# First stage of a spectral filter and mixer kernel: whole folds by class, 32-column rests, and four filters' scans moved into the filter stage

## The chip, the cores and the metric

The kernel runs on one core of a Trainium2 chip. The metric is the device time of one execution in microseconds (us). The kernel before took 1020.65 us, the median of three runs.

## The reference

The input x has S = 2048 tokens (rows) and D = 640 channels (columns). Two kinds of layer alternate, each used twice with the same weights:

```python
def _A_ref(x, w_r, w_i):                 # x: (2048, 640)
    X = rfft2(x)                          # (2048, 321), complex
    X = X * (w_r + 1j * w_i)              # the filter
    return irfft2(X, s=(S, D))
def _B_ref(x, w1, b1, w2, b2):
    h = _layernorm(x)
    u = gelu(einsum("bsd,sf->bdf", h, w1) + b1)     # F = 1728
    return (einsum("bdf,fs->bds", u, w2) + b2).transpose(0, 2, 1)
x = x + _A_ref(_layernorm(x), A_w_r, A_w_i)
x = x + _B_ref(_layernorm(x), ...)
x = x + _A_ref(_layernorm(x), A_w_r, A_w_i)
x = x + _B_ref(_layernorm(x), ...)
```

## The kernel before, in words

The two-dimensional transform is split: along the tokens into 16 × 128 and along the channels into sums and differences of the two halves of a row (a fold), so that cosine and sine tables are multiplied with half as many columns. Values that have to be exact to float32 are held as two float16 numbers, a high and a low part (names that end in h and l), and multiplied in three products (`mm3`).

The stages are written one after the other: `a0_first`, the first stage; `a1`, the filter stage; `a2` and `b1st`, the way back and the first mixer product; then the same for the second layer.

**First stage, `a0_first`.** Sixteen tiles of 128 tokens by 640 channels. For a tile: the statistics of the normalization (`stats`, VectorE: bn_stats twice, then bn_aggr, which writes mv); the centering (`center`, ScalarE, writes one half of zz); a first fold across the row on GpSimd (`diff` and `total`, two instructions of 320 columns on zz); a second fold on VectorE, `adds` and `subs`, which take zz and write F. After it GpSimd copies the end columns that have no partner (`ends`). F is multiplied with the table tm on TensorE in float32 (`product`); tm is the table scaled on ScalarE by the tile's 1/sigma (`scaled`). The result is in PSUM (ps) and split into s1h on ScalarE and s1l on VectorE. A product waits for the copy of the ends, for tm and for s1l of the tile four before it, which frees PSUM. The first four tiles are folded one by one, the other twelve in pairs (m = i // 2). In `product` fill products on a tile of ones (`self.warm`) stand ahead of each pair. An F row is laid out as four blocks of 128 columns and then one block of 128 with four rests of 32: `adds` writes blocks 0 and 3 in one instruction and their rests in a second (helper `each`), `subs` blocks 1 and 2 and their rests. So there are five products of 128 columns a tile, the fifth over all rests.

The filters w (16 groups of 128 x 642 numbers) are loaded in this stage a first time, and ScalarE squares each and sums it (`scan`, tiles jw and xq); the sums give the scale sx.

**Filter stage, `a1`.** Sixteen groups g: the forward product D(g) on TensorE (24 products), its split ph (ScalarE) and pl (VectorE), the row products R and S for two groups at a time, the multiplication with the filter ta and tb (VectorE; they read w and sx), the sums c0 and c1 (GpSimd), xh and xl, the backward products J and I, and the write into Y. From g = 4 on (G0) D needs a stacked operand stk, which is built by transfers through DRAM: s1h and s1l are stored to rest[0] and rest[1] (`store`, line 684), and then read back in another layout (`stack`, lines 690 and 692). The filters are loaded again (`wfetch`, line 698), at most four ahead. `scale_x` makes sx in four steps, on TensorE, VectorE, TensorE and VectorE: the first product (eye, xq) is called X0 here, the second X2.

**What sets the order.** The class `Plan` takes steps with an engine, an assumed duration, the steps that come before, a rank and an earliest time (at), works out an order and issues the instructions in it; VectorE, ScalarE, GpSimd and TensorE keep it. `SEQ1` is the order of TensorE's steps in the filter stage in both layers, written by hand; `SHIFT` moves the rank of single steps. Transfers stand on SyncE's queue in the order that the tile scheduler gives them, behind the semaphores that they need.

Line 56 (58 in the changed kernel) is the wrapper through which all pinned instructions are issued, so nearly all rows of the compute engines bear that line; they are told apart by the tiles.

Of the kernel before, what the change touches and what calls it, by code (L numbers as in the profile page):

```python
# [11 lines left out]
BF16 = mybir.dt.bfloat16  # L12
AF = mybir.ActivationFunctionType
ALU = mybir.AluOpType
# [19 lines left out]
YS = 2.0 ** -14  # L34
PG = 0, 14
WARM = 12, 6
SHIFT = {('y', 1): 2.6, ('xh2', 0): 2.3, ('c0', 1): -1.5, ('w', 1): 2.9, ('xl2', 1): -2.4, ('store', 0): -4.6, ('yh', 0): -2.5, ('yl', 0): 0.4, ('ta', 0): -5.1}
SEQ1 = (
    "D0 D1 S0 D2 D3 D4 S2 I0 D5 I1 S4 D7 I2 D6 I3 S6 D10 I4 D9 D8 I5 "
    "S8 I6 D11 I7 S10 D12 I8 D13 D14 S12 I10 I9 S14 D15 I11 I12 S15 I13 W14 I14 W15 I15"  # L40
)
I32 = mybir.dt.int32
# [97 lines left out]
class Layers:  # L140
# [298 lines left out]
    def a0_first(self, pw):  # L439
# [41 lines left out]
            (eng or G).tensor_tensor(two(e, 1, 161), two(e, 1, 161), two(e, 321, 160), op=ALU.add)  # L481

        def parts(m, q):
            Z, f = zz[m % 3][:, q], F[m][:, q]
            f4 = f[:, :, :512].rearrange("p q (c b) -> p q c b", c=4)
            f5 = f[:, :, 512:].rearrange("p q (c b) -> p q c b", c=4)
            return Z, f, f4, f5

        def each(o, c0, c1, st, Z, lo, hi, op):

            for q in range(o.shape[1]) if o.shape[1] == 1 else (slice(0, 2),):
                V.tensor_tensor(
                    o[:, q, c0:c1:st], Z[:, q, :, lo:hi], Z[:, q, :, 161 + lo:161 + hi], op=op
                )

        def adds(m, q=slice(0, 2)):
            if q.start == 0:
                F[m] = self.t(p, [128, 2, D], F32, "F", 2)
            Z, f, f4, f5 = parts(m, q)
            each(f4, 0, 4, 3, Z, 0, 128, ALU.add)  # L500
            each(f5, 0, 4, 3, Z, 128, 160, ALU.add)

        def ends(m, q=slice(0, 2)):
            Z, f, f4, f5 = parts(m, q)
            G.tensor_copy(f[:, :, 607:640:32], Z.rearrange("p q a b -> p q (a b)")[:, :, 160:802:641])

        def subs(m, q=slice(0, 2)):
            Z, f, f4, f5 = parts(m, q)
# [7 lines left out]
        def product(i):  # L516
            ps = self.big().rearrange("p a b -> p (a b)")
            if i % 2 == 0 and 4 <= i:
                self.warm(ps[:, D:], 10)
            f, t = F[i // 2][:, i % 2], tm.pop(i)  # L520
            for c in (0, 3, 1, 2, 4):
                c = slice(c * 128, c * 128 + 128)
                self.PE.matmul(ps[:, c], f[:, c], t, start=True, stop=True)
            pv[i] = ps[:, :D].rearrange("p (a b) -> p a b", b=8)

        def misc():
            for n in ("eye", "gsel", "b1", "b2"):
# [2 lines left out]
                self.a0_load()  # L530

        def scan(i):
            scans[i] = self.scan_x(pw, i)

        for i in range(2):
            load(i)
# [6 lines left out]
        add = plan.add  # L543
        for i in range(NJ):
            m, last, single = i // 2, i % 2, i < 4
            d = 9 + 2.45 * i
            e = d - 2.45 * (last and not single)
            x0 = None
            if i >= 6:
                x0 = ("x", i)  # L550
                add(x0, "SP", 1.1, [("center", i - 7)], i, load, i, at=8, lag=2.3)
            add(("stats", i), "V", .97, [x0], e - 6.8, stats, i, at=(3.9, 5.0, 8.7, 9.0, 11.0, 12.0)[i] if i < 6 else 0)
            add(("center", i), "T", .75, [("stats", i), ("subs", i - 6)], e - 5.6, center, i)
            add(("diff", i), "G", .85, [("center", i)], e - 4.6, diff, i)
            add(("total", i), *(("G", .85) if i else ("V", .55)), [("diff", i)], e - 3.6, total, i, None if i else V)
            if last:
                add(("var", m), "T", .22, [("stats", i)], e - 4, var, m)
                add(("root", m), "G", .65, [("var", m)], e - 3 - 9 * (m == 0), root, m)
            if single:
                add(("adds", i), "V", .65, [("total", i), ("product", i - 4)], d - 1.4, adds, m, one(i))  # L560
                add(("subs", i), "V", .65, [("adds", i)], d - .8, subs, m, one(i))
                add(("ends", i), "G", .15, [("subs", i)], d - .1, ends, m, one(i))
            elif last:
                k = ("total", i), ("total", i - 1), ("product", i - 4)
                add(("adds", i), "V", .98, k, e - 2.1, adds, m)
                add(("subs", i), "V", .98, [("adds", i)], e - 1.2, subs, m)
# [5 lines left out]
            add(("s1h", i), "T", .6, [("product", i)], 9 + 2.45 * (i + 2), self.a0_s1h_first, i, pv, lag=.2)  # L572
            add(("s1l", i), "V", .74, [("s1h", i)], 10 + 2.45 * (i + 2), self.a0_s1l_first, i, pv)
            add(("w", i), "SP", 1.1, [("scan", i - 5)], i + 6, scan, i, at=8, lag=2.5)
            add(("scan", i), "T", .85, [("w", i)], 22 + 2.45 * i, lambda i=i: scans.pop(i)(), at=12 + 2.1 * i)
# [70 lines left out]
    def a1(self, first):  # L646
# [184 lines left out]
        plan = Plan(4)  # L831
        add = plan.add
        for k in range(2):
            add(("store", k), "SP", .5, [], -2 + k, store, k, at=.8 * k, lag=2.3)
# [4 lines left out]
        for g in range(NG):  # L839
            e = g % 2  # L840
            if g >= G0 and not e:
                add(("stack", g), "SP", 2.3, [("store", 0), ("store", 1), ("D", g - 5)], 0, stack, g, lag=2.3)
            add(("w", g), "SP", .95, [("tb", g - 4)], -2, wfetch, g, lag=2.4)
            add(("D", g), "PE", 1.25 if g >= G0 else 1.8, [("stack", g - e)], 0, forward, g, lag=.2, takes=1)
# [59 lines left out]
        order = [("sx", 0)] * first  # L904
        for q in SEQ1.split():
            k, g = q[0], int(q[1:])
            if g == NG - 1 and k in "SI":
# [976 lines left out]
```

## Time and profile before

| | |
|---|---|
| median of 3 runs | 1020.65 us (1019.9 to 1024.39) |
| the profiled execution | 1022.58 us; span in the profile 1020.8 us |
| TensorE busy | 978.7 us, 96% |
| VectorE, ScalarE, GpSimd busy | 719.0, 593.1 and 250.6 us |
| moved by DMA | 137.05 MB, mean 134 GB/s |
| granted TensorE clock, mean over the span | 0.993 |

A group's row gives line, engine, operation, output <- inputs, shapes and count, then the busy time and the mean of one (ns), then the idle time ahead of it and what ended it. A timeline row gives start and length; instructions that follow one another without a stop are one row, and its length is from the first's start to the last's end. A float32 product leaves two matmul records. PE is TensorE, PEld its loading of the stationary operand, DVE VectorE, ACT ScalarE, POOL GpSimd, SPq SyncE's DMA queue.

### The profile page before, as it was taken

How to read it: one execution, taken by the hardware profiler on the slowest of the kernel's cores; microseconds unless marked ns; L12 is line 12 of the kernel's file. 1: busy time of each engine (PE TensorE's matmuls, PEld its weight loads, DVE VectorE, ACT ScalarE, POOL GpSimd, SP SyncE). 2: the span in 40 equal slices, each digit the busy share in tenths (PEclk: the TensorE clock that was granted, in tenths of full speed). 3: DMA queues.
4: the chain of work that ended last, by engine and by line, in shares of the span. 5: the costliest groups of instructions: out<-in, count | busy, mean ns of one | idle time of the engine just before them, and what ended most of it. 6: DMA issues, size and time to landing. Idle time of an engine off the chain costs nothing. (4 is left out here: it accounts for less than half of the span.)

```text
span 1020.8 us, 21973 instructions
## 1 busy us (share of the span) xinstructions
PE 978.7 (96%) x8873; PEld 725.3 (71%) x8873; DVE 719.0 (70%) x1402; ACT 593.1 (58%) x926; POOL 250.6 (25%) x409
## 2 busy tenths in 40 slices
PE   4789999999999999999998999999999999999998
PEld 3678766677777777777776886667777777777776
DVE  7969877753334867777766796877555664988885
ACT  5858789575555465555542586984544544544541
POOL 6729877100000011111121597850000000000000
PEclk9899999999999999999999999999999999999999
DMA  9765256432222273333324641756222232445411
GB/s 314 231 195 176 74 162 221 151 113 95 83 80 72 71 246 125 130 132 125 128 72 142 174 146 54 223 176 209 88 83 83 73 109 78 144 155 185 154 45 52
DMA packets 54437, 137.05 MB, mean 134 GB/s; under 512 B 6440, under 2 KB 11456, under 8 KB 54336
## 3 DMA queue, kind: packets, MB, share of 16 engines
q1 hardware_dynamic: 54336, 135.66, 41.1%
q8 instruction: 69, 1.13, 0.5%
q14 instruction: 32, 0.26, 0.1%
HBM read 112.57 MB, written 23.07 MB: 133 GB/s over the span
## 5 line engine op out<-in xcount | busy, mean ns | idle before, releaser
L56 PEld LDWEIGHTS <-wh 128*128 128x128 f16 x2992 | 289.9, 98 | 114.2 <-issue 3.3
L56 PEld LDWEIGHTS <-wl 128*128 128x128 f16 x1616 | 158.0, 98 | 61.5
L56 PE MATMUL ps<-hh,wh 128*128 128x320 f16 x896 | 186.5, 299 | 1.6 <-ACT hh L56 1.6
L56 PE MATMUL ps<-hl,wh 128*128 128x320 f16 x896 | 184.7, 299 | 0.0
L56 PE MATMUL ps<-hh,wl 128*128 128x320 f16 x832 | 171.4, 299 | 0.0
L56 DVE SCALAR_TENSOR_TENSOR wl<-raw,s,wh 128x1024 f16<-128x1024 f32 (+2 forms) x88 | 110.5, 1273 | 47.0 <-ACT wh L56 46.9
L56 PE MATMUL ps<-uh,wl 128*128 128x320 f16 x448 | 133.1, 299 | 0.0
L56 PE MATMUL ps<-ul,wh 128*128 128x320 f16 x448 | 133.1, 299 | 0.0
L56 ACT ACTIVATE wh<-raw,s 128x1024 f16<-128x1024 f32 (+2 forms) x92 | 94.9, 1050 | 65.2 <-PE ps L56 58.5
L56 PE MATMUL ps<-uh,wh 128*128 128x320 f16 x416 | 124.3, 299 | 0.0
L56 ACT ACTIVATE junk<-raw 128x896 bf16<-128x896 f32 (+1 forms) x60 | 59.7, 995 | 44.8 <-DMA raw<-w 44.3
L56 PE MATMUL ps<-u,wo 128*128 128x320 f16 x504 | 69.9, 299 | 0.0
L56 DVE TENSOR_TENSOR xt<-xt,ps 128x320 f32<-128x320 f32 (+1 forms) x96 | 45.0, 490 | 30.7 <-ACT ec L56 20.3
L56 POOL TENSOR_TENSOR r<-v,mh 128x1 f32<-128x1 f32 (+1 forms) x56 | 33.5, 599 | 125.6 <-DVE nm L56 112.6
L56 PEld LDWEIGHTS <-wo 128*128 128x128 f16 x504 | 49.3, 98 | 19.1
L56 DVE BATCH_NORM_STATS2 st<-xt 128x6 f32<-128x320 f32 x128 | 56.3, 481 | 3.9 <-DMA xt<-x 3.2
L56 PE MATMUL ps<-tm,F 128*128 128x128 f32 x160 | 30.1, 345 | 21.8 <-ACT tm L56 13.5
L56 PE MATMUL ps<-tDi,yh 128*128 128x322 f16 x240 | 50.2, 299 | 0.0
L56 DVE TENSOR_SCALAR qt<-ps 128x1 f32<-128x1 f32 x14 | 2.1, 154 | 66.5 <-PE ps L56 66.5
L56 PE MATMUL ps<-u,wh 128*128 128x320 f16 x336 | 48.4, 299 | 0.0
L56 PE MATMUL ps<-u,wl 128*128 128x320 f16 x336 | 48.3, 299 | 0.0
L56 PE MATMUL ps<-tD,s1h 128*128 128x160 f16 (+1 forms) x320 | 45.1, 246 | 2.5 <-ACT s1h L56 1.3
(177 smaller groups left out, 1855.4 us busy)
## 6 DMA issues: line engine op xcount, KB each, us to landing
raw<-w SPq DMA_DIRECT2D x56, 512.0 KB
xt<-x SPq DMA_DIRECT2D x80, 320.0 KB
w<-w SPq DMA_DIRECT2D x48, 321.0 KB
x<-xt SPq DMA_DIRECT2D x48, 320.0 KB
raw<-w SPq DMA_DIRECT2D x32, 448.0 KB
raw<-w2z SPq DMA_DIRECT2D x32, 448.0 KB
out<-xt SPq DMA_DIRECT2D x15, 320.0 KB
stk<-rest SPq DMA_DIRECT2D x36, 64.0 KB
```

What stands on the lines that cost most here:

```text
L56: i = f(*a, **k)
```

## The change

1. The layout of F becomes four blocks of 160 columns. `adds` then writes blocks 0 and 3 in one instruction and `subs` blocks 1 and 2 in another. The shorter assumed durations and the step of 2.2 instead of 2.45 us a tile change the plan's order.
2. `product` multiplies the first 128 columns of each block as before, and the last 32 of each block by themselves, into partitions 32c to 32c + 31 of the fifth block of ps: eight products a tile instead of five. Eight fill products instead of ten stand ahead of a pair, and 24 (`LASTW`) after the last tile's product.
3. Only filters 4 to 15 are loaded and scanned in the first stage (`NQ0` = 4). The squares of filters 0 to 3 are taken in the filter stage (`square`, steps q), from the loads that this stage makes anyway; sx waits for them, and the stack of filter 4 for those loads.
4. `SEQ1` begins with D0 D1 X0 D2 X2 S0 instead of (sx first) D0 D1 S0 D2; X0 and X2 exist in the first layer only.

```diff
+LASTW = 24
+NQ0 = 4
-SHIFT = {('y', 1): 2.6, ...
+SHIFT = {('q', 0): -4, ('q', 1): -4, ('y', 1): 2.6, ...
 SEQ1 = (
-    "D0 D1 S0 D2 D3 D4 S2 I0 D5 ...
+    "D0 D1 X0 D2 X2 S0 D3 D4 S2 I0 D5 ...
...
-        def each(o, c0, c1, st, Z, lo, hi, op):
+        def each(o, Z, op):
             for q in range(o.shape[1]) if o.shape[1] == 1 else (slice(0, 2),):
-                V.tensor_tensor(
-                    o[:, q, c0:c1:st], Z[:, q, :, lo:hi], Z[:, q, :, 161 + lo:161 + hi], op=op
-                )
+                V.tensor_tensor(o[:, q], Z[:, q, :, 0:160], Z[:, q, :, 161:321], op=op)
...
-            each(f4, 0, 4, 3, Z, 0, 128, ALU.add)
-            each(f5, 0, 4, 3, Z, 128, 160, ALU.add)
+            each(f[:, :, 0::3], Z, ALU.add)
...
-            each(f4, 1, 3, 1, Z, 0, 128, ALU.subtract)
-            each(f5, 1, 3, 1, Z, 128, 160, ALU.subtract)
+            each(f[:, :, 1:3], Z, ALU.subtract)
...
-                self.warm(ps[:, D:], 10)
+                self.warm(ps[:, D:], 8)
-            for c in (0, 3, 1, 2, 4):
-                c = slice(c * 128, c * 128 + 128)
-                self.PE.matmul(ps[:, c], f[:, c], t, start=True, stop=True)
+            for c in (0, 3, 1, 2):
+                self.PE.matmul(ps[:, c * 128:c * 128 + 128], f[:, c * 160:c * 160 + 128], t, start=True, stop=True)
+            for c in range(4):
+                a = c * 160 + 128
+                self.PE.matmul(ps[c * 32:c * 32 + 32, 512:D], f[:, a:a + 32], t, start=True, stop=True)
...
+            if i == NJ - 1:
+                self.warm(self.big()[:, 1], LASTW)
...
-            d = 9 + 2.45 * i
+            d = 9 + 2.2 * i
...
+            if i < NG - NQ0:
+                add(("w", i), "SP", 1.1, [("scan", i - 5)], i + 6, scan, i, at=8, lag=2.5)
+                add(("scan", i), "T", .85, [("w", i)], 22 + 2.2 * i, lambda i=i: scans.pop(i)(), at=12 + 2.1 * i)
...
+        def square(g):
+            junk = self.t(p, [128, 2, NL], BF16, "jw", 1)
+            T.activation(junk, w[g], AF.Square, accum_out=self.xq[:, g:g + 1])
...
+            for g in range(NQ0):
+                add(("q", g), "T", .85, [("w", g)], 0, square, g, at=.6)
-            steps("sx", (.4, .5, .4, 1.1), ("PE", "V", "PE", "V"), 0, self.scale_x(p, at), [], (0, 3))
+            steps("sx", (.4, .5, .4, 1.1), ("PE", "V", "PE", "V"), 0, self.scale_x(p, at), [("q", g) for g in range(NQ0)], (0, 3))
```

VectorE in the middle of the first stage of the kernel before, one pair of tiles (st and mv are the statistics, F the folds of the pair, s1l the low parts of two earlier tiles):

```order
L56 BN_STATS st_446<-xt_323 128x6 x2
L56 BN_AGGR mv_85_449<-st_446 128x2
L56 TENSOR_TENSOR F_456<-zz_8_160 128x2x2x128
L56 TENSOR_TENSOR F_456<-zz_8_160 128x2x2x32
L56 BN_STATS st_466<-xt_350 128x6 x2
L56 BN_AGGR mv_85_449<-st_466 128x2
L56 TENSOR_TENSOR s1l_143<-ps_395,s1h_142 128x160x4
L56 TENSOR_TENSOR F_456<-zz_8_160 128x2x256
L56 TENSOR_TENSOR F_456<-zz_8_160 128x2x64
L56 TENSOR_TENSOR s1l_143<-ps_427,s1h_142 128x160x4
```

The same place in the changed kernel:

```order
L58 BN_STATS st_428<-xt_327 128x6 x2
L58 BN_AGGR mv_81_431<-st_428 128x2
L58 BN_STATS st_455<-xt_356 128x6 x2
L58 BN_AGGR mv_81_431<-st_455 128x2
L58 TENSOR_TENSOR F_463<-zz_8_160 128x2x2x160
L58 TENSOR_TENSOR s1l_143<-ps_395,s1h_142 128x160x4
L58 TENSOR_TENSOR F_463<-zz_8_160 128x2x320
L58 TENSOR_TENSOR s1l_143<-ps_433,s1h_142 128x160x4
```

Four fold instructions a pair are two, and the second statistics stand ahead of the first fold.

ScalarE at the end of the first stage, before (jw is the scan of a filter, ph the first split of the filter stage):

```order
L56 ACTIVATE s1h_142<-ps_633 128x160x4
L56 ACTIVATE jw_545,xq<-w_543 128x642
L56 ACTIVATE jw_596,xq<-w_594 128x642
L56 ACTIVATE s1h_142<-ps_662 128x160x4
L56 ACTIVATE jw_603,xq<-w_601 128x642
L56 ACTIVATE s1h_142<-ps_673 128x160x4
L56 ACTIVATE s1h_142<-ps_692 128x160x4
L56 ACTIVATE junk,sqs<-b1s 128x14
L56 ACTIVATE ph_804<-ps_741 128x2x321
```

The same place after:

```order
L58 ACTIVATE jw_533,xq<-w_531 128x642
L58 ACTIVATE s1h_142<-ps_652 128x160x4
L58 ACTIVATE s1h_142<-ps_670 128x160x4
L58 ACTIVATE s1h_142<-ps_689 128x160x4
L58 ACTIVATE junk,sqs<-b1s 128x14
L58 ACTIVATE jw_773,xq<-w_761 128x642
L58 ACTIVATE jw_803,xq<-w_767 128x642
L58 ACTIVATE jw_812,xq<-w_765 128x642
L58 ACTIVATE jw_839,xq<-w_769 128x642
L58 ACTIVATE ph_841<-ps_778 128x2x321
```

No scan stands between the last three s1h now, and four squares stand behind them, ahead of ph.

SyncE's queue between the two stages, before (rest are the stores of s1h and s1l, stk the stacked operand):

```order
L1089 DMA raw_955<-w 128x1024
L698 DMA w_766<-w 128x642
L698 DMA w_812<-w 128x642
L698 DMA w_825<-w 128x642
L684 DMA rest_139_734<-s1h_142 128x2048
L684 DMA rest_139_735<-s1l_143 128x2048
L698 DMA w_913<-w 128x642
L690 DMA stk_773<-rest_139_734 32x4x256
```

The same place after:

```order
L1098 DMA raw_979<-w 128x1024
L698 DMA w_761<-w 128x642
L698 DMA w_765<-w 128x642
L698 DMA w_767<-w 128x642
L698 DMA w_769<-w 128x642
L684 DMA rest_132_759<-s1h_142 128x2048
L684 DMA rest_132_760<-s1l_143 128x2048
L953 DMA tDi_749<-tDi 128x3864
L690 DMA stk_806<-rest_132_759 32x4x256
```

The fourth filter load now stands ahead of the stores, and tDi, a table for the way back, ahead of the first stack; before it stood three stacks later.

More of the change, by code (lines that the diff above doesn't have):

```diff
@@ L498, in adds @@
                 F[m] = self.t(p, [128, 2, D], F32, "F", 2)
-            Z, f, f4, f5 = parts(m, q)
-            each(f4, 0, 4, 3, Z, 0, 128, ALU.add)
-            each(f5, 0, 4, 3, Z, 128, 160, ALU.add)
+            Z, f = parts(m, q)
+            each(f[:, :, 0::3], Z, ALU.add)
         def ends(m, q=slice(0, 2)):
-            Z, f, f4, f5 = parts(m, q)
-            G.tensor_copy(f[:, :, 607:640:32], Z.rearrange("p q a b -> p q (a b)")[:, :, 160:802:641])
+            Z, f = parts(m, q)
+            G.tensor_copy(f[:, :, 2:4, 159], Z.rearrange("p q a b -> p q (a b)")[:, :, 160:802:641])
         def subs(m, q=slice(0, 2)):
-            Z, f, f4, f5 = parts(m, q)
-            each(f4, 1, 3, 1, Z, 0, 128, ALU.subtract)
-            each(f5, 1, 3, 1, Z, 128, 160, ALU.subtract)
+            Z, f = parts(m, q)
+            each(f[:, :, 1:3], Z, ALU.subtract)
         def scaled(i):
@@ L532, in scan @@
         def scan(i):
-            scans[i] = self.scan_x(pw, i)
+            scans[i] = self.scan_x(pw, i + NQ0)
         for i in range(2):
@@ L545, in a0_first @@
             m, last, single = i // 2, i % 2, i < 4
-            d = 9 + 2.45 * i
-            e = d - 2.45 * (last and not single)
+            d = 9 + 2.2 * i
+            e = d - 2.2 * (last and not single)
             x0 = None
@@ L559, in a0_first @@
             if single:
-                add(("adds", i), "V", .65, [("total", i), ("product", i - 4)], d - 1.4, adds, m, one(i))
-                add(("subs", i), "V", .65, [("adds", i)], d - .8, subs, m, one(i))
+                add(("adds", i), "V", .5, [("total", i), ("product", i - 4)], d - 1.4, adds, m, one(i))
+                add(("subs", i), "V", .5, [("adds", i)], d - .8, subs, m, one(i))
                 add(("ends", i), "G", .15, [("subs", i)], d - .1, ends, m, one(i))
@@ L564, in a0_first @@
                 k = ("total", i), ("total", i - 1), ("product", i - 4)
-                add(("adds", i), "V", .98, k, e - 2.1, adds, m)
-                add(("subs", i), "V", .98, [("adds", i)], e - 1.2, subs, m)
+                add(("adds", i), "V", .84, k, e - 2.1, adds, m)
+                add(("subs", i), "V", .84, [("adds", i)], e - 1.2, subs, m)
                 add(("ends", i), "G", .2, [("subs", i)], e - .1, ends, m)
@@ L571, in a0_first @@
             add(("product", i), "PE", 2.2, [("ends", i), ("scaled", i), ("s1l", i - 4)], i, product, i)
[L572 to L575, printed above, removed]
+            add(("s1h", i), "T", .6, [("product", i)], 9 + 2.2 * (i + 2), self.a0_s1h_first, i, pv, lag=.2)
+            add(("s1l", i), "V", .74, [("s1h", i)], 10 + 2.2 * (i + 2), self.a0_s1l_first, i, pv)
+            if i < NG - NQ0:
+                add(("w", i), "SP", 1.1, [("scan", i - 5)], i + 6, scan, i, at=8, lag=2.5)
+                add(("scan", i), "T", .85, [("w", i)], 22 + 2.2 * i, lambda i=i: scans.pop(i)(), at=12 + 2.1 * i)
             if i in (1, 2, 3):
@@ L833, in a1 @@
         for k in range(2):
-            add(("store", k), "SP", .5, [], -2 + k, store, k, at=.8 * k, lag=2.3)
+            add(("store", k), "SP", .5, [], -2 + k, store, k, at=.7 + .8 * k, lag=2.3)
         last = NG - 2
@@ L841, in a1 @@
             if g >= G0 and not e:
-                add(("stack", g), "SP", 2.3, [("store", 0), ("store", 1), ("D", g - 5)], 0, stack, g, lag=2.3)
-            add(("w", g), "SP", .95, [("tb", g - 4)], -2, wfetch, g, lag=2.4)
-            add(("D", g), "PE", 1.25 if g >= G0 else 1.8, [("stack", g - e)], 0, forward, g, lag=.2, takes=1)
+                add(("stack", g), "SP", 2.3, [("store", 0), ("store", 1), ("D", g - 5)] + [("w", i) for i in range(4) if g == G0], 0, stack, g, lag=2.3)
+            early = first and g < NQ0
+            add(("w", g), "SP", .05 if early else .95, [("tb", g - 4)], -2, wfetch, g, lag=0 if early else 2.4)
+            add(("D", g), "PE", 1.25 if g >= G0 else 1.8, [("stack", g - e)], 0, forward, g, at=1.2, lag=.2, takes=1)
             add(("ph", g), "T", .61, [("D", g), ("S", row(max(g - 4, 0))) if g >= 4 else None], 0, phi, g)
@@ L903, in a1 @@
             add(("zl", t), "V", .33, [("z", t)], 1, begin, t, 1)
-        order = [("sx", 0)] * first
+        order = []
         for q in SEQ1.split():
             k, g = q[0], int(q[1:])
-            if g == NG - 1 and k in "SI":
+            if k == "X":
+                order += [("sx", g)] * first
+            elif g == NG - 1 and k in "SI":
                 order += [(k, g, t) for t in range(3)]
```

9 lines of the change are left out of this document (3 added, 6 removed).

## The prediction

> **What bounds the kernel now.** I read the page's first part for the whole, the windows for single stages, the timeline for one pair of tiles and for the stage's end, and the groups by form for prices.
>
> ```profile
> span 1020.8 us, 21973 instructions
> PE 978.7 (96%) x8873; PEld 725.3 (71%) x8873; DVE 719.0 (70%) x1402; ACT 593.1 (58%) x926; POOL 250.6 (25%) x409
> ```
>
> TensorE fills 96% of the span, so nothing done on another engine pays where TensorE is full. The windows (length, then busy time by engine, granted clock, DMA share and GB/s) show where it is not.
>
> ```profile
> core 0: us, PE busy (x) PEld busy (x) DVE busy (x) ACT busy (x) POOL busy (x), PEclk, DMA share, GB/s
> 10.00:20.00 10.00, 7.06 (x29) 6.22 (x29) 9.86 (x26) 7.19 (x15) 7.82 (x12) 1.00 1.04 398
> 32.94:38.88 5.94, 4.53 (x32) 4.14 (x33) 5.87 (x13) 5.11 (x12) 4.64 (x7) 0.82 0.45 126
> 38.88:44.83 5.95, 3.59 (x32) 3.02 (x32) 5.88 (x13) 5.17 (x12) 4.65 (x7) 1.00 0.80 238
> 100.00:110.00 10.00, 10.00 (x235) 8.70 (x228) 10.00 (x15) 9.55 (x22) 8.65 (x13) 1.00 0.33 92
> ```
>
> The two middle rows are one pair of tiles each: VectorE is busy 5.9 of 5.95 us, TensorE 3.6 and 4.5. The first stage is VectorE's; from 100 us on TensorE is full. So an edit pays up to about 75 us, and only there. One pair in the timeline (start, length):
>
> ```profile
> 33.97 0.88 DVE L56 TENSOR_TENSOR F<-zz 128x512 f32<-128x512 f32 x2
> 34.09 0.83 ACT L56 ACTIVATE zz<-xt,mv 128x640 f32<-128x640 f32 x1 [0.67 <-DVE mv L56]
> 34.77 0.88 DVE L56 BATCH_NORM_STATS2 st<-xt 128x6 f32<-128x320 f32 x2
> 34.99 3.08 POOL L56 TENSOR_TENSOR zz<-zz 128x320 f32<-128x320 f32 x3 [0.91 <-ACT zz L56]
> 36.49 1.73 DVE L56 TENSOR_TENSOR F<-zz 128x512 f32<-128x512 f32 x2
> 38.15 0.81 DVE L56 TENSOR_TENSOR s1l<-ps,s1h 128x640 f16<-128x640 f32 x1
> 38.50 0.87 POOL L56 TENSOR_TENSOR zz<-zz 128x320 f32<-128x320 f32 x1
> ```
>
> A fold is two pieces, 512 and 128 columns. With GpSimd idle both take 0.80 us (33.97 to 34.77); beside GpSimd's operations the same two take 1.66 (36.49 to 38.15), 0.86 more, about one GpSimd operation (0.87 alone, at 38.50). The groups of the first 62 us (busy us, mean ns):
>
> ```profile
> L56 DVE TENSOR_TENSOR F<-zz 128x512 f32<-128x512 f32 x12 | 8.8, 737 | 0.0
> L56 DVE TENSOR_TENSOR F<-zz 128x128 f32<-128x128 f32 x12 | 7.4, 618 | 0.0
> L56 DVE TENSOR_TENSOR F<-zz 128x256 f32<-128x256 f32 x8 | 4.0, 494 | 0.0
> L56 DVE TENSOR_TENSOR F<-zz 128x64 f32<-128x64 f32 x8 | 4.4, 550 | 0.0
> L56 POOL TENSOR_TENSOR zz<-zz 128x320 f32<-128x320 f32 x31 | 30.1, 977 | 12.1 <-ACT zz L56 11.6
> L56 ACT ACTIVATE jw<-w 128x642 bf16<-128x642 f32 x16 | 11.7, 733 | 0.2
> L56 ACT ACTIVATION_READ_ACCUMULATOR jw<-w 128x1 f32 x16 | 3.0, 189 | 0.0
> ```
>
> The short pieces cost nearly what the long ones do (618 against 737 ns for a quarter of the columns). By columns alone the 0.80 us splits into about 0.6 and 0.2, so the short piece waits some 0.4 us on the mean and the long one 0.15: GpSimd gets in between the two.
>
> **The change, part by part.** The profiled execution took 1022.58 us, 1.93 above the median 1020.65; I sum against the first and take 1.93 off.
>
> *Whole folds, pairs.* A whole fold is one instruction of 640 columns. The subtraction s1l, also of 640 columns, takes 0.78 to 0.81 (38.15; two in 1.56 in the tail below) with one operand in PSUM; I take 0.73 for the fold, 0.07 off the two pieces. VectorE's work of a pair becomes 5.94 − 0.80 − 1.66 + 2 × 0.73 = 4.94 us, plus 0.15 per fold if it waits like the long piece: 5.24. ScalarE is then the next: 5.11 to 5.17 busy plus a remnant of the 0.67 it waits for the second statistics, say 0.2, gives 5.35. GpSimd's 4.65 stays below. TensorE: below. So 5.95 becomes 5.35, five pairs, −3.0 us (0.6 per pair). Ends: no gain if each fold waits as both pieces did (0.56; VectorE 6.06); −4.2 if ScalarE's remnant goes and the outer pairs shrink to VectorE's 5.1.
>
> *Whole folds, the first four tiles.*
>
> ```profile
> 12.36 2.21 POOL L56 TENSOR_TENSOR zz<-zz 128x320 f32<-128x320 f32 x2 [1.73 <-ACT zz L56]
> 22.61 1.37 POOL L56 TENSOR_TENSOR zz<-zz 128x320 f32<-128x320 f32 x1 [0.46 <-ACT zz L56]
> 22.58 1.54 DVE L56 TENSOR_TENSOR F<-zz 128x512 f32<-128x512 f32 x2
> ```
>
> Eight pieces of 64 columns, 4.4 us of VectorE, go into the eight of 256. But until the first pair's fold at 22.58 GpSimd works from 12.36 to 22.15 (0.46 before 22.61) without a stop, about ten operations. What they can give is what they lose beside VectorE now, 977 − 870 ns each, 1.07 us, and a part of the 1.73 that GpSimd waits before 12.36 for a centering, behind VectorE's statistics. I take half of that, so −2.0; ends −1.0 and −2.6 (most of it). The last pair's folds:
>
> ```profile
> 51.51 1.68 DVE L56 TENSOR_TENSOR F<-zz 128x512 f32<-128x512 f32 x4
> 51.94 0.72 PE L56 MATMUL ps<-ones 128*128 128x128 bf16 x10
> 53.35 0.19 POOL L56 COPY F<-zz 128x4 f32<-128x4 f32 x1 [1.42 <-DVE F L56]
> 52.50 2.70 PE L56 MATMUL ps<-tm,F 128*128 128x128 f32 x20
> 55.32 0.73 ACT L56 ACTIVATE jw<-w 128x642 bf16<-128x642 f32 x1
> 56.04 1.28 ACT L56 ACTIVATE s1h<-ps 128x640 f16<-128x640 f32 x2
> 56.76 1.56 DVE L56 TENSOR_TENSOR s1l<-ps,s1h 128x640 f16<-128x640 f32 x2 [0.49 <-ACT s1h L56]
> 58.37 0.39 PE L56 MATMUL ps<-eye,xq 128*16 128x128 f32 x2 [3.17 <-DVE s1l L56]
> ```
>
> 1.68 becomes 2 × 0.73: −0.2. The last copy then ends near 53.54 − 5.2 = 48.3.
>
> *Rests of 32 columns.* 20 records in 2.70 are ten fp32 products, 0.27 each. Per tile one product of 128 columns becomes four of 32. Their price is not in the trace: between a quarter (0.07, four rests together as dear as the one) and 0.27 each. I take 0.13, since a product streams the same 128 columns whatever stands in the array, but the four write different quarters. Per pair TensorE then has 8 × 0.27 + 8 × 0.13 plus eight fills (ten take 0.72): 3.8 us, hidden under 5.35; at 0.27 it is 4.9, still hidden at full clock.
>
> *The tail.* Behind the last copy stand now six products, then a scan (55.32) and both s1h; s1l ends at 58.32. Without the scan the last s1h would end at 55.98 instead of 57.32, −1.3; the rests give back 0.4 (ten products of which eight are rests: 0.54 + 1.04 + hand-overs, against 1.66). −0.9; ends 0 and −1.4.
>
> *Scans moved.* Four scans (0.92 each with their read) leave ScalarE's first stage and become squares on loads that the filter stage makes anyway: four loads of 321 KB less, while ScalarE has 3.7 us more after the last s1h. The scale sx now waits for the four squares, and its first product X0 stands on TensorE between D1 and D2. The loads 1 to 3 wait for the last copy (48.3) and should land about 3 us on, as the last s1h ends (51.7); the squares end at 55.4. D0 starts at 52.5 (tail), so X0 is wanted at 56.1: 0.7 spare, and what the loads are late beyond it TensorE waits. Behind the squares on ScalarE stands ph of filter 0, for which pl and R wait; it comes some 0.9 later than now, while TensorE has D1, X0 and D2, 3.6 us. So 0; without that cover +0.9. Queued behind the loads on SP are the two rests and the stacks: rival three.
>
> *Order and fills at the start of the filter stage.*
>
> ```profile
> 58.70:63.87 5.17, 5.17 (x50) 5.04 (x49) 1.32 (x3) 0.71 (x1) 0.00 (x0) 0.67 0.78 264
> 67.11:71.83 4.72, 4.72 (x70) 4.55 (x72) 4.38 (x6) 1.83 (x3) 2.76 (x4) 1.00 0.38 96
> 66.44 0.74 PE L56 MATMUL ps<-pl,tS 64*64 64x321 f16 x14 [0.48 <-DVE qb L56]
> 74.07 0.40 PE L56 MATMUL ps<-tI,xh 64*128 64x128 f16 x8 [0.47 <-DVE pl L56]
> ```
>
> D0 and D1, 48 products, ran at a clock of 0.67 after the wait of 3.17 us. The second window's rate, 0.074 each, makes them 3.54: −1.63 if the 24 fills (0.072 each, 1.7 us) keep the clock. [...] D2 in front of S0 also takes the place of the stops around S0 (0.48 and more): from D0 to the end of D2 (67.11 + 24 × 0.074 = 68.9) it is 10.2 us now; then 72 × 0.074 + 0.2 for X0 and X2 + 2.2 for R0 and S0 (S0 takes 0.74, R0 has twice its products) + 0.5 of waits = 8.2. Together −1.95; at the lost clock −0.3. Given back: between S0 and I0 (74.07) TensorE no longer has D2's 1.8 us, and the chain ta, tb, c0, c1, xh does not shorten; I take half, +0.9 (0 to 1.8).
>
> *Second filter stage.* It gets the order too, D2 before S0.
>
> ```profile
> PE ps L56 <- DMA stk<-rest: 1.2, 1, 1.2
> ```
>
> TensorE's longest wait there is 1.2 us for a stack; it ends when the stack lands, whatever was done before, so nothing is gained: 0, from −1.2 to +3 (two filter loads of 321 KB more ahead of the stacks, 2.4 us each at the page's mean of 134 GB/s, less the 1.2).
>
> Sum: −2.0 − 3.0 − 0.2 − 0.9 − 1.95 + 0.9 = −7.15; 1022.58 − 7.15 = 1015.4, on the median **1013.5 us**.
>
> **The rivals.** *One: GpSimd takes back the folds.* Each whole fold waits 0.56, as both pieces do now; VectorE stays at 6.06 a pair, (6.06 − 5.35) × 5 = 3.5 back: 1017.0. For it: GpSimd has as much to do in less time. Against: the long pieces wait only 0.15.
>
> *Two: the rests make TensorE the bound.* With 0.27 a rest a pair is 4.9 us of TensorE, and at the clock of 0.82, by the two rows of a pair, 4.9 × 4.53 / 3.59 = 6.2. The clock is not always there; at 5.95 the 3.0 us of the pairs are gone: 1016.5. [...] Against it: TensorE has 1.4 to 2.4 us free in a pair.
>
> *Three, slower than before: the stacks come late.* In the new order tDi stands ahead of the stack of filters 4 and 5, which D4 awaits.
>
> ```profile
> tDi<-tDi SPq DMA_DIRECT2D x1, 966.0 KB
> rest<-s1h SPq DMA_DIRECT2D x1, 512.0 KB
> DMA packets 54437, 137.05 MB, mean 134 GB/s; under 512 B 6440, under 2 KB 11456, under 8 KB 54336
> ```
>
> From the last copy on three loads (963 KB), two rests (1024) and tDi move first: 2953 KB. D4 is wanted some 14.2 us after the copy: D0 at 5.16 − 0.9 (53.54 to 58.70 now), then the 8.2 above and D3's 1.8. At the mean 134 GB/s they take 22.0, and D4 is 7.8 late: 1021.3. It decides below 2953 / 14.2 = 208 GB/s; the rows of such stretches say 238 and 264 GB/s. A lateness of up to 2 us lies in my range.
>
> That the folds are not fewer is excluded: the order has 20 where there were 40.
>
> **How the numbers follow.** Forecast 0.60 (own range 1010 to 1016.5), one 0.17, two 0.14, three 0.09. The range runs from 1009.5, the forecast with the long ends of folds and tail, to 1018.0, which holds one and two with half a term lost; outside are rival three and little else. About 0.5%, 5.1 us, is what a measurement of this kernel can tell; below 1015.5 lie nine tenths of the forecast and a third of rivals one and two: 0.64. Slower than 1025.8 needs rival three and a lost clock: 0.03. The rest is 0.33.
>
> **What would show it.** Right: pairs of 5.2 to 5.5 us, whole folds at 0.73 to 0.9; last copy at 48 to 49; D0 within 4.5 us of it, at a clock over 0.9; no stop of TensorE before D4 over 1 us. Rival one: whole folds of 1.2 and more; two: products back to back through the pair at a clock below 0.9; three: TensorE waiting for the stack, with tDi just landed. I am wrong if the pairs still take 5.8 or more, or if the filter stage gives back over 3 us.

## The result, and the profile after

The changed kernel takes 1010.38 us, the median of six runs (1009.7 to 1010.79); the kernel before 1021.56 us in the six runs beside it. The ratio is 0.9884 with a 95% interval from 0.9869 to 0.9899: 10 to 13 us faster. The profiled execution took 1010.17 us, 12.4 less than the one of before.

Two pairs of tiles of the first stage in the windows view of the changed kernel, then D0 and D1 of the first and of the second layer:

```profile
core 0: us, PE busy (x) PEld busy (x) DVE busy (x) ACT busy (x) POOL busy (x), PEclk, DMA share, GB/s
29.81:34.74 4.93, 4.08 (x43) 2.90 (x42) 4.86 (x11) 4.53 (x10) 4.93 (x7) 1.00 0.70 217
34.74:39.67 4.93, 3.99 (x43) 2.90 (x42) 4.86 (x12) 4.81 (x11) 4.93 (x7) 1.00 0.92 279
50.65:54.19 3.54, 3.54 (x49) 3.41 (x49) 0.76 (x1) 2.68 (x7) 0.00 (x0) 1.00 1.00 310
549.96:553.52 3.56, 3.56 (x48) 3.39 (x49) 1.13 (x3) 0.71 (x1) 0.00 (x0) 1.00 0.93 269
```

A pair takes 4.93 us, not 5.95. VectorE is busy 4.86 of it, GpSimd 4.93 and ScalarE 4.5 to 4.8: three engines are full or nearly so at once. Both windows of D0 and D1 are at the full clock.

VectorE and GpSimd in the timeline of one pair:

```profile
29.81 0.78 DVE L58 TENSOR_TENSOR F<-zz 128x640 f32<-128x640 f32 x1
30.26 3.36 POOL L58 TENSOR_TENSOR zz<-zz 128x320 f32<-128x320 f32 x3
30.51 0.82 DVE L58 TENSOR_TENSOR s1l<-ps,s1h 128x640 f16<-128x640 f32 x1
31.24 0.81 DVE L58 TENSOR_TENSOR F<-zz 128x640 f32<-128x640 f32 x1
31.98 0.82 DVE L58 TENSOR_TENSOR s1l<-ps,s1h 128x640 f16<-128x640 f32 x1
32.71 0.88 DVE L58 BATCH_NORM_STATS2 st<-xt 128x6 f32<-128x320 f32 x2
33.70 0.87 POOL L58 TENSOR_TENSOR zz<-zz 128x320 f32<-128x320 f32 x1
34.74 0.78 DVE L58 TENSOR_TENSOR F<-zz 128x640 f32<-128x640 f32 x1
```

The instruction behind a whole fold starts 0.70 to 0.74 us after it: in these pairs a fold does not wait for GpSimd. It is GpSimd that waits, three of its operations taking 3.36 us where three of 0.87 would take 2.6.

That depends on where GpSimd stands. In the fifth pair the second fold follows the first directly and starts while GpSimd is at work:

```profile
40.13 2.46 POOL L58 TENSOR_TENSOR zz<-zz 128x320 f32<-128x320 f32 x2
40.36 1.49 DVE L58 TENSOR_TENSOR F<-zz 128x640 f32<-128x640 f32 x1
```

There a whole fold does wait, some 0.7 us (1.49 for 0.78).

The groups of the first 62 us:

```profile
L58 DVE TENSOR_TENSOR F<-zz 128x640 f32<-128x640 f32 x12 | 10.3, 868 | 0.9 <-POOL zz L58 0.9
L58 DVE TENSOR_TENSOR F<-zz 128x320 f32<-128x320 f32 x8 | 4.6, 614 | 0.0
L58 POOL TENSOR_TENSOR zz<-zz 128x320 f32<-128x320 f32 x31 | 31.2, 1024 | 6.4 <-ACT zz L58 6.3
```

All folds are 14.9 us of VectorE, where the four forms of before were 24.6; the mean of 868 ns holds the one long fold of the fifth pair. The end of the stage, in the timeline:

```profile
19.82 0.83 DVE L58 TENSOR_TENSOR F<-zz 128x640 f32<-128x640 f32 x1 [0.51 <-POOL zz L58]
44.41 1.56 DVE L58 TENSOR_TENSOR F<-zz 128x640 f32<-128x640 f32 x2 [0.36 <-POOL zz L58]
46.12 0.19 POOL L58 COPY F<-zz 128x4 f32<-128x4 f32 x1 [1.10 <-DVE F L58]
45.51 3.02 PE L58 MATMUL ps<-tm,F 128*128 128x128 f32 x32 [0.33 <-ACT tm L58]
48.60 0.70 ACT L58 ACTIVATE s1h<-ps 128x640 f16<-128x640 f32 x1 [0.36 <-PE ps L58]
```

The first pair's fold stands at 19.82 (22.58 before), the last pair's at 44.41 (51.51), and D0 at 50.65 (58.70). So 8.05 us are gained when the filter stage starts, 9.96 when its last product ends (114.11 for 124.07), nothing between the two filter stages, and 2.5 more from the stops ahead of the second layer's filter stage to that stage's end. The profiles differ by 12.4 us and the medians by 11.2.

### The profile page after: what moved, and what is told of

It is laid out like the page before. It is cut to its first block, busy times and chain, and to the rows that moved or that the text cites. A ratio compares the mean times of both kernels' runs of the same rounds, so it can differ in the third digit from the quotient of the medians.

```text
span 1008.4 us, 22169 instructions
## 1 busy us (share of the span) xinstructions
PE 976.7 (97%) x8981; PEld 718.1 (71%) x8981; DVE 710.3 (70%) x1382; ACT 592.2 (59%) x926; POOL 251.6 (25%) x409
## 5 line engine op out<-in xcount | busy, mean ns | idle before, releaser
L58 PE MATMUL ps<-tm,F 128*128 128x128 f32 (+1 forms) x256 | 30.5, 317 | 15.0 <-ACT tm L58 11.5
```

The source lines that it names most:

```text
L58: i = f(*a, **k)
```

## The experiments

The first theory is that of the folds: VectorE set the pair, and the whole folds shortened it. Its rivals were the scans (ScalarE was the engine relieved), the plan's new numbers, and for the filter stages the clock against the order of TensorE's steps and the transfers. Each experiment has its own runs of the kernel before; ratios are to those.

**All sixteen scans in the first stage again.**

```diff
-NQ0 = 4
+NQ0 = 0
```

> The changed kernel with all sixteen scans back in the first stage (no squares in the filter stage). The folds' theory (the first stage's gain comes from VectorE, whose pair of tiles fell to its own sum of 4.93 us): pairs stay at 4.9 to 5.2 us, the four scans only lengthen ScalarE's tail, and the time is 0.5 to 1.5 us above the changed kernel's. The scans' theory (ScalarE is the engine that the change relieved): pairs go back to 5.35 us or more, 3 us or more above.

Measured: 1015.22 us, ratio 0.9930 (0.9914 to 0.9945), some 4.8 us above the changed kernel. The pairs are 4.92 us, the same; the folds' theory was right on that and the scans' theory wrong. But the four scans cost far more than the 0.5 to 1.5 us that I expected, behind the pairs. ScalarE's tail in the timeline:

```profile
48.30 0.74 ACT L58 ACTIVATE jw<-w 128x642 bf16<-128x642 f32 x1
49.04 0.68 ACT L58 ACTIVATE s1h<-ps 128x640 f16<-128x640 f32 x1
49.62 0.73 ACT L58 ACTIVATE jw<-w 128x642 bf16<-128x642 f32 x1
50.47 0.74 ACT L58 ACTIVATE jw<-w 128x642 bf16<-128x642 f32 x1
51.21 0.69 ACT L58 ACTIVATE s1h<-ps 128x640 f16<-128x640 f32 x1
```

The waits of TensorE there (us in total, times, longest), and D0 and D1 in the windows:

```profile
PE ps L58 <- DVE s1l L58: 2.9, 1, 2.9
```
```profile
53.24:58.17 4.93, 4.93 (x48) 4.72 (x47) 0.83 (x1) 0.71 (x1) 0.00 (x0) 0.70 1.01 353
```

Two scans stand ahead of the last s1h, D0 comes 2.6 us later (53.24), and after a stop of 2.9 us D0 and D1 run at a clock of 0.70, 1.4 us more, in spite of the 24 fills ahead of the stop. That makes 4.3 us by the end of the first filter stage; the second layer, whose D0 and D1 ran at a lower clock here too (5.16 us), adds 0.8 in the profile. So the scans' part of the change is worth some 4.8 us in a place where no pair shows it, and part of that is the clock.

**Folds in two pieces again.**

```diff
-                V.tensor_tensor(o[:, q], Z[:, q, :, 0:160], Z[:, q, :, 161:321], op=op)
+                for u, v in ((0, 128), (128, 160)):
+                    V.tensor_tensor(o[:, q, :, u:v], Z[:, q, :, u:v], Z[:, q, :, 161 + u:161 + v], op=op)
```

> The changed kernel with each fold in two pieces again (128 and 32 columns of each block). The folds' theory: the second pieces wait for GpSimd again, pairs go from 4.93 to 5.8 or 6.0 us, and with the first four tiles the time is 5 to 8 us above the changed kernel's. The scans' theory, and that of the plan's new numbers: less than 2 us above, pairs at 5.2 us or below.

Measured: 1019.02 us, ratio 0.9971 (0.9959 to 0.9983), 8.6 us above the changed kernel, beyond the upper end. The groups of its pieces, and one pair in the windows:

```profile
L58 DVE TENSOR_TENSOR F<-zz 128x128 f32<-128x128 f32 x12 | 8.7, 729 | 0.0
L58 DVE TENSOR_TENSOR F<-zz 128x512 f32<-128x512 f32 x12 | 8.7, 722 | 0.0
```
```profile
28.69:35.11 6.42, 5.69 (x59) 3.91 (x58) 6.35 (x13) 5.16 (x11) 5.23 (x6) 0.91 0.63 199
```

A piece of 128 columns now takes as long as one of 512, and a pair takes 6.42 us, more than the 5.95 of before. In the new order both folds of a pair stand beside a busy GpSimd and take 1.53 and 1.55 us (before, the first stood in GpSimd's idle time and took 0.80). The folds' theory stands, and the expectation was too low: the new order makes pieces dearer than they were.

**Whole folds alone, in the kernel before** (the new `parts`, `each`, `adds`, `ends`, `subs` and the products of the changed kernel; scans, numbers, fills and order as before).

> The kernel before with whole folds, the layout of four times 160 columns and the products of 32 columns alone; scans, plan's numbers, fills and order as before. The folds' theory: pairs of 5.0 to 5.4 us, 5 to 7 us below the kernel before. The theory of the plan's new numbers and the scans': pairs stay at 5.6 us or more, less than 3 us below.

Measured: 1015.17 us, ratio 0.9935 (0.9921 to 0.9950), 6.6 us below the kernel before. A pair:

```profile
30.40:35.79 5.39, 3.89 (x45) 2.98 (x44) 5.32 (x11) 5.34 (x13) 4.76 (x7) 1.00 0.49 138
```

ScalarE is busy 5.34 of 5.39: in the old order it is full, as I had forecast for the changed kernel. VectorE is full too, at 5.32, with second folds of 1.0 to 1.2 us in three of the pairs; which of the two sets the pair no run takes apart. The five pairs take 25.7 us here (first fold at 20.47, last pair's at 46.20) and 24.6 in the changed kernel; the rest of the pairs' gain, 1.1 us, comes with the new order, in which both statistics stand ahead of the folds.

**Which engine sets the 4.93 us?** One kernel leaves out the statistics over the second 320 columns of a tile, the other half the columns of GpSimd's total.

```diff
-            s1 = self.stats1(p, x[i])
+            s1 = self.t(p, [128, 1, 6], F32, "st", 2)
+            V.bn_stats(s1[:, 0], x[i][:, :320])
```
```diff
-            (eng or G).tensor_tensor(two(e, 1, 161), two(e, 1, 161), two(e, 321, 160), op=ALU.add)
+            a, b = two(e, 1, 161), two(e, 321, 160)
+            (eng or G).tensor_tensor(a[:, :, :80], a[:, :, :80], b[:, :, :80], op=ALU.add)
```

> The changed kernel with statistics over the first 320 columns of each tile only (left out: the second half's), 0.9 us of VectorE's pair. If VectorE's own sum sets the pair (4.93 us): pairs fall to ScalarE's 4.7 us or less, the stage ends 1.2 to 2.5 us earlier. If GpSimd does (it is busy 10.00 of 10 us): pairs stay at 4.9 us, less than 0.7 us earlier.

> The changed kernel with GpSimd's total over half of its columns (left out: the other half), about 0.85 us of GpSimd's pair. If VectorE's own sum sets the pair: pairs stay at 4.9 us and the time within 0.7 us of the changed kernel's, apart from the first tiles. If GpSimd does: pairs fall to 4.7 us or less, 1.2 us or more earlier.

Measured: 1009.89 us (0.9884; 0.9863 to 0.9905) and 1009.07 us (0.9876; 0.9851 to 0.9901). A pair with half the statistics:

```profile
29.38:34.22 4.84, 3.97 (x43) 2.87 (x42) 4.17 (x8) 4.73 (x11) 4.84 (x7) 1.00 0.63 207
```

and one with half the total:

```profile
29.08:34.01 4.93, 4.18 (x43) 2.92 (x41) 4.86 (x12) 4.53 (x10) 4.34 (x6) 1.00 0.68 220
```

With 0.6 us less on GpSimd the pair stays at 4.93: VectorE sets it. With 0.7 less on VectorE the pair falls by 0.09 only, since GpSimd is full at 4.84; the first expectation's 4.7 was missed for that reason. In its middle pairs the stage is balanced within 2%: an edit to one engine brings next to nothing there. Its ends are not: with half the total D0 comes 1.2 us sooner (49.46), of which 0.6 is gained ahead of the first pair and 0.4 in the fifth, more than the 0.7 that I allowed.

**No fills behind the last product** (`LASTW = 0`).

> The changed kernel without the 24 fill products behind the last tile's product. If the fills keep the clock: D0 and D1 take about 5.2 us at a clock below 0.9, and the time is 1.6 us above the changed kernel's. The rival, that the wait ahead of D0 (now about 2.1 us in all) is too short to lose the clock: D0 and D1 stay at 3.6 us, 0 to 0.3 us above.

Measured: 1011.44 us, ratio 0.9892 (0.9876 to 0.9908). In the profile D0 and D1 keep the full clock over a stop of 1.7 us (the waits, then the windows):

```profile
PE ps L58 <- ACT jw L58: 1.7, 1, 1.7
```
```profile
50.59:54.14 3.55, 3.55 (x49) 3.41 (x49) 0.77 (x1) 2.69 (x7) 0.00 (x0) 1.00 1.02 342
```

The rival holds for this execution. It took 1009.76 us, the three others 1011.2 to 1011.7; whether those lost the clock at this place no trace shows. So the fills' worth in the changed kernel is not shown. Nor does the length of a stop by itself say what comes: in the run with the folds alone D0 and D1 kept the clock (3.56 us) behind a stop of 2.6, and in the second layer of the kernel before they lost it (0.67) behind three of 1.34 at the most. The last section comes back to the clock.

**The same fills, in the kernel before.** The 24 fills behind the last tile's product, nothing else.

> The kernel before with the 24 fill products behind the last tile's product and nothing else; the stop ahead of D0 falls from 3.17 to about 1.6 us. If the clock is lost by the length of the stop: D0 and D1 fall from 5.17 to 3.6 us and S0, which waits for ph and pl of both, comes 1.0 to 1.6 us sooner, the time is 0.5 to 1.6 us below the kernel before. If it is lost by the whole stage's work: D0 and D1 stay above 4.5 us, within 0.3 us.

Measured: 1023.45 us, ratio 0.9998 (0.9984 to 1.0011), no change. The first half came true; D0 and D1, and a later stretch, in the windows, and TensorE's longest wait in that stretch:

```profile
58.62:62.18 3.56, 3.56 (x50) 3.43 (x49) 1.32 (x3) 0.71 (x1) 0.00 (x0) 1.00 0.98 339
622.00:628.00 6.00, 4.25 (x17) 2.40 (x18) 1.06 (x4) 1.50 (x4) 1.25 (x2) 0.56 0.37 109
```
```profile
PE ps L56 <- DVE Y2l L56: 1.9, 1, 1.9
```

With a stop of 0.99 us instead of 3.17 the clock is kept, and S0 and all that follows comes 1.7 us sooner. At the end of the second filter stage the lead is some 3 us (621.87 for 624.92): the stop ahead of its D0 is 0.95 us instead of 1.34, and TensorE's wait of 1.2 us there, of which more below, did not come. At 622 us a new stop of 1.9 us and a clock of 0.56 take it all back. No instruction changed its place there. The fills take one more PSUM tile in the first stage, and in the built kernel the first product of the second layer's way back then waits for the split of Y2 (Y2h, Y2l), where before it waited for an older product only: the tiles behind the added one have moved on by one place. That this is the cause is read from the built kernel and was not tried by itself; the changed kernel takes that tile too and has no such stop. The fills are worth 1.7 us in the first layer, and the stop hides it in the total.

**TensorE's order** (S0 ahead of D2 again, in one layer at a time).

```diff
-        for q in SEQ1.split():
+        for q in (SEQ1 if first else SEQ1.replace('D2 X2 S0', 'S0 X2 D2')).split():
```

> The changed kernel with S0 ahead of D2 again in the second layer's filter stage alone. The order's theory: the stop of TensorE ahead of R0 (0.6 us before) comes back and nothing behind it is covered, 0.5 to 1.0 us above the changed kernel's; the other 1.6 us that this stage lost in the profile of before were the clock (D0 and D1 at 5.16 us), which the order does not touch. The rival, that the order is worth the whole 2.5 us of this stage: 2 us or more above.

> The changed kernel with S0 and X2 ahead of D2 in the first layer's filter stage alone. The order's theory: R0 waits for ph of group 1 and X2 for xb, 0.5 to 1.2 us above the changed kernel's. The rival, that D2 only moves work TensorE does later anyway and the chain to I0 sets the time: 0 to 0.2 us above, or below.

Measured: 1010.94 us (0.9896; 0.9872 to 0.9920) and 1010.97 us (0.9897; 0.9875 to 0.9918). In the first layer the filter stage is 0.7 us longer with the old order, in the profile, as the order's theory had it; the times can't tell that from nothing. In the second layer the stage ends 1.1 us later, but D0 and D1 ran at a lower clock:

```profile
549.91:554.98 5.07, 5.07 (x49) 4.94 (x50) 1.12 (x3) 0.71 (x1) 0.00 (x0) 0.68 0.93 313
```

That is 1.5 us by itself, ahead of the point where the order differs. So the order is worth no measurable time there, and another cause for the second layer's 2.5 us was needed.

**The second layer's transfers.** In the kernel before, one filter load more ahead of the first stack:

```diff
-                add(("stack", g), "SP", 2.3, [("store", 0), ("store", 1), ("D", g - 5)], 0, stack, g, lag=2.3)
+                add(("stack", g), "SP", 2.3, [("store", 0), ("store", 1), ("D", g - 5)] + [("w", i) for i in range(2) if g == G0 and not first], 0, stack, g, lag=2.3)
```

> The kernel before with one change: in the second layer the filter load of group 1 stands ahead of the first stack in SyncE's queue, not behind it. The theory that D4 waits there for a bank of PSUM which tb of group 1 gives back, and tb's ta for this load (not for the stack): ta of group 1 follows tb of group 0 without a wait, D4 comes 1.2 us or more nearer to D0 than 12.55 us, and the stage is 1 to 2 us shorter. The rival, that the stack itself is what D4 waits for: D4 stays at 12.5 us after D0 or comes later, 0 to 0.5 us slower.

Measured: 1020.99 us, ratio 0.9980 (0.9969 to 0.9991), 0.9 to 3.2 us faster. VectorE and TensorE around D4 in the kernel before:

```profile
569.00 0.88 DVE L56 SCALAR_TENSOR_TENSOR tb<-ps,sx,w 128x642 f32<-128x642 f32 x1
571.15 0.89 DVE L56 SCALAR_TENSOR_TENSOR ta<-ps,sx,w 128x642 f32<-128x642 f32 x1 [1.27 <-DMA w<-w]
571.95 0.88 DVE L56 SCALAR_TENSOR_TENSOR tb<-ps,sx,w 128x642 f32<-128x642 f32 x1
572.89 0.32 PE L56 MATMUL ps<-tD,s1h 128*128 128x160 f16 x2 [1.20 <-DMA stk<-rest]
```

and with the load moved:

```profile
568.89 0.89 DVE L56 SCALAR_TENSOR_TENSOR ta<-ps,sx,w 128x642 f32<-128x642 f32 x1
569.69 0.88 DVE L56 SCALAR_TENSOR_TENSOR tb<-ps,sx,w 128x642 f32<-128x642 f32 x1
570.62 0.32 PE L56 MATMUL ps<-tD,s1h 128*128 128x160 f16 x2
572.12 0.23 PE L56 MATMUL ps<-tD,stk 96*128 96x160 f16 x1 [1.11 <-DMA stk<-rest]
```

Before, D4's first product is one of s1h, which needs no stack; it starts at 572.89, when the second tb ends (571.95 + 0.88 = 572.83). It waited for the PSUM that tb gives back, tb for its ta, and ta 1.27 us for its filter load, which stood in SyncE's queue behind the first stack. The profile names the stack as the releaser, and that is wrong here: the trace has the last landing of that stack at 569.7. With the load first, ta and D4 start without a wait, and now the stack itself holds D4, whose first product on it comes 11.0 us after D0 instead of 12.8. The stage is 1.7 us shorter from D0 to its last product (64.58 to 62.84).

Not all of that is the load's. D0 and D1 ran at 0.67 before and at 1.00 here. In the runs with the folds alone and with the fills in the kernel before, D0 and D1 of the second layer lost the clock as well (5.15 and 4.94 us), the queue has the old order, and yet ta did not wait; the stage took 63.72 and 63.53. By them the wait is worth about 1 us, and it does not come in every execution. What SyncE's first stack waited for ahead of it tells the two cases apart:

```profile
SPq L690 <- DMA rest<-s1l: 3.8, 1, 3.8
SPq L685 <- DMA rest<-s1l: 1.7, 1, 1.7
SPq L692 <- DMA rest<-s1l: 1.4, 1, 1.4
```

These are the kernel before, the folds alone and the fills in the kernel before. The stack waits for the store of s1l, and the load behind it came late where the store landed late; why it does so in some executions is not shown. The times fit a cost that is paid in some: the kernel before took 1020.25 to 1026.23 us in 23 executions, the one with the load first 1019.69 to 1021.73 in twelve.

The opposite, the changed kernel with the second layer's transfers in the old order (the first stack no longer behind the loads, and the earliest times of that layer's first store and of its products D as before):

> The changed kernel with the second layer's transfers in the order of before (the first stack ahead of two of the filter loads); TensorE's order there stays the new one. The theory that the stack's landing sets the start of that stage: D4 comes 11 to 12.6 us after D0 as before (now 9.7), and the time is 1.5 to 2.8 us above the changed kernel's. The rival, that the 2.5 us there were the clock and the order of TensorE: D4 stays at 9.7 to 10.2 us after D0, 0 to 0.5 us above.

Measured: 1015.44 us, ratio 0.9933 (0.9918 to 0.9948), 5 us above. D4 was not late, 9.1 us after D0: that half of the expectation failed. The waits of TensorE in its second filter stage and just behind:

```profile
PE ps L58 <- DVE tb L58: 2.2, 1, 2.2
PE ps L58 <- DVE Y2l L58: 1.9, 1, 1.9
```

The first is the filter load again (the stack waited 3.4 us for the store, ta 2.0 for its load, and R of groups 2 and 3 for the PSUM behind tb): 1.4 us at the end of the stage. The second is the stop on Y2 that the fills in the kernel before had as well; what brings it here was not tried. It and the clock behind it (0.85 and 0.87 in the windows 612:618 and 618:624) make 3.2 more, and 0.4 were lost ahead of the first D0. So this run shows the load's wait, and its total is not the price of it.

**More fills in the second layer**, over the stops ahead of D0 (12 behind the last products of the mixer's last tile, 78 instead of 64 ahead of them).

> The changed kernel with 12 fill products more between the last tile of the mixer and D0 of the second layer, and 78 for 64 ahead of that tile's products, over stops of 0.95 and 1.2 us. If the loss of the clock there is what sets apart the slower of the runs: no profile and no run loses it, the median falls by 0.3 to 1.0 us and the spread shrinks. If the stack's landing covers it: no change, within 0.3 us.

Measured: 1010.52 us, ratio 0.9886 (0.9868 to 0.9904), no change. The fills wait 0.9 us themselves for s1l, whose place in PSUM they use, and push D0 back by 0.9; the stack then waits less. Of the kernels here that leave nothing out, none is faster than the changed one.

## Why the prediction was right, and where it was not

The forecast was 1015.4 for the profiled execution; it took 1010.17. Of the gain, 7.15 us were forecast and 12.4 came in the profile, 11.2 between the medians. The range held the median of 1010.38, but with some luck: the long ends of folds and tail, which were to make its lower end of 1009.5, reach 1011.2 only (1013.5 − 1.2 − 0.6 − 0.5). Two of the signs named for being right were passed on the better side, pairs of 4.93 us for 5.2 to 5.5 and the last copy at 46.1 for 48 to 49. By its steps:

- *Whole folds, pairs.* The mechanism held; the size was off. I put −3.0 and ScalarE as the next bound at 5.35; it is −4.3 (22.58 to 51.51 before, 19.82 to 44.41 now). 5.35 was right for the old order, as the run with the folds alone shows (ScalarE 5.34). I had the new order before me, with both statistics ahead of the folds, and left its effect out.
- *Whole folds, first four tiles.* −2.8 instead of −2.0, at the upper end: GpSimd's chain began 1.35 us sooner (11.01 for 12.36), and the fold ended closer behind it.
- *The last folds and the tail.* −0.1 and −0.8 for −0.2 and −0.9: D0 stands 4.34 us behind the last copy. Sixteen products took 3.02 us; with 0.27 for each of the eight wide ones a rest of 32 columns costs 0.11, below the 0.13 that I took. Rival two is out. No run here shows what a change between the wide and the narrow products costs by itself; the sum leaves no room for much.
- *Scans moved.* No time was lost behind them: the squares ran to 52.7, ph followed, and TensorE went from D1 through X0 and D2 without a stop. What I did not see is that at the new pace the scans would otherwise have stood in the tail, for 4.8 us.
- *Order and fills at the start of the filter stage.* −2.4 for −1.95, with D0 and D1 at the full clock (3.54 us). The give-back was 0.5, not 0.9. That the fills kept the clock, as the sum has it, is not shown for the changed kernel: without them it was kept as well (1.00 behind a stop of 1.7 us). In the kernel before they shortened the stop from 3.17 to 0.99 us, and the clock was 1.00 instead of 0.67.
- *Second filter stage.* Here the working failed: "it ends when the stack lands, whatever was done before, so nothing is gained". The wait of 1.2 us was not for the stack; it was for PSUM and, at its root, for a filter load behind the stack in the queue. The two loads that I priced as a risk, up to +3, cost at most the 0.5 us that TensorE now waits for the stack, and the stage gained 2.5 in the profile. Of these, 0.4 are the shorter stop ahead of D0 (0.95 us in every kernel here that takes the fills' tile, except the one with more fills there, and 1.34 in the three that don't). The load's wait is about 1 by the runs above. The rest goes, as far as the profiles show, with the clock of D0 and D1, lost in the profile of before (5.16 us) and kept in this one (3.56): that part is luck of the two executions, and no run says how much of the 1.6 us reaches the stage's end.

Rival one, GpSimd taking back the folds, came in the fifth pair only; elsewhere in the pairs a whole fold takes 0.78 to 0.90 us. It is alive in the run with the pieces, at 6.42 us a pair. Rival three did not come either: D4 starts its stack product at 60.26, 9.6 us after D0, without a stop.

## What to carry to other kernels

Where two engines get in each other's way, count instructions as well as columns, and look at which engine starts first: here a second short piece cost as much as the long one (0.73 and 0.72 us), a whole fold that started just ahead of GpSimd's next operation cost next to nothing extra (0.81 for 0.78), and one that started behind it cost 0.7 us more (1.49). A wait that the profile puts down to a transfer is worth a look at the waiting instruction's operands; if it does not read the transfer's tile, look for the memory it writes and who frees that. And an edit to one stage can come with a new wait hundreds of microseconds later, so a run's time is read beside its stages.

## What the runs showed of the hardware that was not expected

**Short pieces against GpSimd.** With the folds in pieces 128 columns took 0.73 us beside a busy GpSimd, as long as 512 (0.72). In the changed kernel a whole fold of 640 that starts at 31.24, just ahead of GpSimd's next operation (31.28), takes 0.81, and that operation 1.51 instead of 0.87; the fold that starts at 40.36, behind one begun at 40.13, takes 1.49 itself.

**The clock and short stops.** The stops ahead of the second layer's D0 (1.2, 0.37 and 0.95 us, within some 4 us) are the same in ten profiles; D0 and D1 ran at the full clock in six of them (3.55 us) and at about 0.7 in four (4.94 to 5.16). It is 1.4 to 1.6 us each time, more than several edits of this study are worth. In the trace of the kernel before the granted clock is 0.50 for 3.41 us four times (from 31.68, 45.34, 58.99 and 560.75 us), in that of the changed kernel once, for 6.83 (from 16.03); the full stretches between the four are 10.24, 10.24 and 498.35 us, each a multiple of 3.41. Two pieces of 3.41 us in the run with the old order in the second layer, the second of them at half the clock, then two of the changed kernel, counted on from its one loss:

```profile
546.33:549.74 3.41, 1.19 (x15) 0.84 (x15) 2.19 (x8) 1.78 (x4) 0.00 (x0) 1.00 0.92 308
549.74:553.15 3.41, 3.24 (x25) 3.27 (x26) 0.46 (x3) 0.00 (x0) 0.00 (x0) 0.50 0.88 264
545.10:548.52 3.42, 1.85 (x31) 1.51 (x29) 2.81 (x9) 1.01 (x2) 0.38 (x2) 1.00 0.89 236
548.52:551.93 3.41, 2.46 (x37) 2.28 (x35) 1.02 (x4) 0.78 (x3) 0.00 (x0) 1.00 0.92 317
```

In the first run all but a little of the three stops lies in one piece; TensorE is busy 35% of it, and the next is at half the clock. In the changed kernel the stops are divided between two (54% and 72%), and the clock stays. The kernel before, divided in the same way, has TensorE busy 47% of the piece ahead of its second layer's D0:

```profile
557.34:560.75 3.41, 1.60 (x21) 1.29 (x22) 2.03 (x6) 1.21 (x4) 0.00 (x0) 1.00 0.53 213
560.75:564.16 3.41, 3.41 (x29) 3.41 (x27) 0.00 (x0) 0.71 (x1) 0.00 (x0) 0.50 0.96 287
```

The pieces ahead of its three earlier losses (from 28.27, 41.92 and 55.58 us) have 45, 44 and 18%, that ahead of the changed kernel's loss (from 12.62) 43%. The changed kernel and the run with the old order have the same three stops there, and D0 and D1 took 3.56 us behind them in the one and 5.07 in the other. Why the clock falls is not shown: no run here moves the stops against these pieces on purpose.
